# Two open heads' sums in the last periods, eight fill halves a period, a sixth early heads' step, half routing pieces, and two late weights in free buffers

## The chip, the cores and the metric

The kernel runs on one core of a Trainium2 chip. The metric is the device time of one execution in microseconds. TensorE is PE here, VectorE DVE, ScalarE ACT, GpSimd POOL; SP is the queue that issues the DMAs. PE reads its operands from SBUF and writes the eight PSUM banks, each of 128 x 512 float32: three score banks st0 to st2, four banks sm0 to sm3, and one bank dn.

## The reference

Input x has 2048 tokens of 512 features. Two branches are mixed by a gate per token:

```python
g = sigmoid((x * gate_w).sum(-1, keepdims=True))
qkv = (x @ wqkv).reshape(B, S, 3, 32, 16).transpose(2, 0, 3, 1, 4)     # 32 heads of 16
p = softmax(einsum("bhqd,bhkd->bhqk", q, k) * 16 ** -0.5)
a = merge(einsum("bhqk,bhkd->bhqd", p, v)) @ wo                         # attention
b = (sigmoid(x @ w_gate) * (x @ w_up)) @ w_down                         # GLU, 1792 hidden
out = g * a + (1 - g) * b
```

## The kernel before

Every matrix product is made of three matmuls on high and low parts of the operands (`terms`), which makes it exact enough in the fast number format. The instructions of PE, ACT, DVE and POOL run in the order in which the program writes them; SP's order is set by a scheduler.

The main loop (L891) has 256 periods, numbered k. In each, PE does eight score matmuls (`st_part`, L679, four "t0" for the period and four "t1" for the next), whose exponentials ACT takes (L681), eight matmuls for the row maxima of later scores (L292, "m0", "m1"), which DVE reduces (L294), twelve halves of a "fill" sum, and at the end the values (`values`, L831): probabilities times v, 16 records in the trace. The bank of the values is copied by ACT, in the last eleven periods by DVE (L838), and POOL adds the copy to a running sum (L848). A string of words, STEADY, gives the order in a period.

A fill sum (class `Sum`) is work that has nothing to do with the scores: the GLU's products, and towards the end the **early heads' steps**. A sum's operands have 128 rows, but each matmul of it takes only 64 of them, the lower or the upper half of PE's rows ("d0" and "d1"), so that it runs beside a score matmul, which uses the other half of the rows. [...]

From k = 245 on no row maxima are left, and the order is

```python
LAST = "t0 d1 t0 d1 t0 d1 turn t0 t1 t1 d0 t1 d0 t1 d0"
```

six halves a period. Scores and values take their banks from a ring of seven (`bank7`), the open fill sum is in dn, and DVE copies finished sums out (L469). There are EARLY = 5 steps of the last projection (attention output times wo) of which the first half of the heads, k-chunks 0 and 1 of 4, is summed in this way: ten sums of 12 halves, stored as `hp` (L515) and loaded back in the final stage.

Beside this, three more things hang in the main loop. The routing logits (`logits`, L818): 16 DVE instructions of 128 x 512, each multiplying 128 rows of x with the gate weights and summing, two in every six periods from k = 75 to 122; the rows of x are loaded by `logit_load` (L814). The denominators (L789 reciprocals on DVE), one in each period from k = 192 to 211. The first two chunks of the GLU's gate (`hidden_early`, L757), exponentials on ACT in k = 242 to 245.

The final stage (from L1011) is the GLU's down projection: 28 chunks of 24 matmuls (L1021) at about 0.227 us, four banks at a time (`bankt`, the first is dn), with eight heads' steps between them (`heads_out`): 4 k-chunks for steps that were not begun early, 2 for those that were. The values of k = 255 stand behind the first 12 down matmuls. The weights w_down are loaded late (`late_raw`), two row blocks at a time into a ring of two buffers, and split into high and low parts by ACT and POOL (L101, L104; `wd_h`, `wd_l`).

Of the kernel before, what the change touches and what calls it, by code (L numbers as in the profile page):

```python
# [12 lines left out]
F32 = mybir.dt.float32  # L13
# [25 lines left out]
FREE = NPER - LEAD // 2  # L39
EARLY = 5  # L40
WARM = 9
# [5 lines left out]
def gated_mix(ctx, tc, x, xT, wqk, wv, wo, w_gate, w_up, w_down, gate_w, out):  # L47
# [103 lines left out]
    class Sum:  # L151


        def __init__(self, o, ab):
            self.o, self.n, self.last, self.token = o, 0, None, None
            self.ops = list(terms(ab))
            self.left = [list(self.ops), list(self.ops)]
# [230 lines left out]
    def filling():  # L388
# [87 lines left out]
        def sums_of(kind, n, ws):  # L476
# [93 lines left out]
        for job, nxt in zip(jobs, jobs[1:]):  # L570
            kind, n = job
            coming = None
            for at, run in enumerate(sums_of(kind, n, ws)):
# [7 lines left out]
                if job == ("chain", pairs[-1]):  # L581
# [3 lines left out]
                    if at in (6, 7):  # L585
                        first_heads_split(at - 6)
                if kind == "heads" and at in (2, 4, 6):
                    if at == 2:
                        first_heads_load(4)
                    first_heads_split(at // 2 + 1)  # L590
# [126 lines left out]

    def late_raw(src, r):
        raw = keep.tile([P, 2, D], F32, name=f"late{r}", tag="ev", bufs=2)
        sp.dma_start(raw, src[r * P:(r + 2) * P, :].rearrange("(k p) d -> p k d", p=P))  # L720
        return raw

    def down_late(f, raw):
        if f < 6:
            th, tl, bufs = ("wh", "wl", 4) if f < 4 else ("sum", "part", 2)
            for a in range(2):
                if f + a == 5:
                    th = tl = "wr"
                h = keep.tile([P, D], F32R, name=f"wd{f + a}h", tag=th, bufs=bufs)
                l = keep.tile([P, D], F32R, name=f"wd{f + a}l", tag=tl, bufs=bufs)  # L730
                split(h, l, raw[:, a, :], act, pool)
                wd.append((h, l))
        else:
            fs = slice(f - 6, f - 4)
            split(wd_h[:, fs, :], wd_l[:, fs, :], raw, act, pool)
            wd.extend((wd_h[:, f - 6 + a, :], wd_l[:, f - 6 + a, :]) for a in range(2))
# [78 lines left out]

    def logits(t, a):
        xn = tok[t][:, a, :]
        dve.tensor_tensor_reduce(xn, xn, gwb, scale=1.0, scalar=0.0, op0=ALU.mult, op1=ALU.add,  # L818
                                 accum_out=logit[:, t + a:t + a + 1])

# [31 lines left out]
    def mx(b):  # L852
        for j in range(LEAD, NSTEP):
# [6 lines left out]
            denominators(1, 32, 64, 2)]  # L860
    run = next(fill)

    def dense(g):
        while run:
            run.half(g)
            yield

    spot = []

    def emit(order, **parts):  # L870

        for word in order.split():
            if word == "turn":
                if run:
                    turn(run)
# [8 lines left out]
    SUMS = 0  # L884
    LAST = "t0 d1 t0 d1 t0 d1 turn t0 t1 t1 d0 t1 d0 t1 d0"

# [4 lines left out]
    for k in range(NPER):  # L891
        n = 2 * k
        if n + LEAD == NSTEP:
            bank = bank7
            leave = dve.tensor_copy
        if 75 <= k < 123:
# [13 lines left out]
        if run and run.done():  # L910
            run = next(fill, None)
        elif run and run.n:
            turn(run)
        for half in list(mrow):
            later[:0] = put_max(half)
        work(2.6)
        later.extend(soon)
# [158 lines left out]
```

## Time and profile before

| | |
|---|---|
| median of 3 runs | 1687.64 us (1687.16 to 1688.01) |
| profiled execution | 1688.48 us |
| its span in the trace | 1686.7 us |
| TensorE clock granted | 0.999 |
| PE, DVE, ACT, POOL busy | 100%, 86%, 81%, 56% of the span |

The span runs from the first to the last recorded instruction; 1.78 us of the execution lie around it. Starts and durations in the rows of the trace are in us from the span's start. In a row such as `514.70 1.91 PE L831 MATMUL sm<-p,v ... x16`, the first number is the start, the second how long it (or the run of 16 alike) took, and `sm<-p,v` says that a bank of the sm kind is written from the tiles p and v.

### The profile page before, as it was taken

Reading aid. Unit: us, or ns where it says so; the run is one execution under the profiler, and the core shown is the slowest. Engines: PE = TensorE matmul, PEld = TensorE weight load, DVE = VectorE, ACT = ScalarE, POOL = GpSimd, SP = SyncE. Lnnn points to the kernel's source line nnn. Section 1 sums busy time; section 2 is a strip of 40 time slices with the busy share of each in tenths; the row PEclk is TensorE's granted clock in tenths of the full one; section 3 lists DMA queues with packets and bytes.
Section 4 is the critical chain, followed back from the end, with each engine's and each line's share of the span. In section 5 each row is a group of like instructions: output and inputs, shape, how many; then the busy total and the mean of one; then the engine's idle time right before and its main releaser. Section 6 shows DMA issues by size and latency. Waiting matters only on the chain.

```text
span 1686.7 us, 34636 instructions
## 1 busy us (share of the span) xinstructions
PE 1679.6 (100%) x12485; PEld 1027.2 (61%) x12485; DVE 1451.5 (86%) x2347; ACT 1362.6 (81%) x2657; POOL 938.9 (56%) x920
## 2 busy tenths in 40 slices
PE   9999999999999999999999999999999999999999
PEld 7755555555555555555555555555555555568887
DVE  7988888888889999999888888889998888787653
ACT  4188898988988898889898888989888988985331
POOL 1134476647666666566666766666666667543110
PEclk9999999999999999999999999999999999999999
DMA  7511457366565554555635353434343535368862
GB/s 237 148 46 59 127 175 210 133 164 208 145 197 133 166 156 151 163 162 182 165 102 146 102 145 107 137 104 132 104 129 113 133 110 171 109 208 285 290 200 70
DMA packets 143755, 254.19 MB, mean 151 GB/s; under 512 B 24224, under 2 KB 36512, under 8 KB 140704
## 3 DMA queue, kind: packets, MB, share of 16 engines
q1 hardware_dynamic: 135968, 237.30, 46.6%
q10 hardware_dynamic: 7616, 14.68, 2.8%
q8 instruction: 98, 1.61, 0.4%
q14 instruction: 73, 0.60, 0.1%
HBM read 149.42 MB, written 102.50 MB: 149 GB/s over the span
## 4 chain that ended last, share of the span: by engine, by line
PE 97%; DMA 1%; POOL 1%; issue 0%; ACT 0%; DVE 0%; SPq 0%; POOLq 0%; DVEq 0%
PE dn L162 30%; PE sm L831 27%; PE sm L292 13%; PE st L679 7%; PE sm L679 5%; PE sm L1021 4%; PE st L292 2%; PE st L162 2%; PE dn L1021 2%; PE st L1021 1%; PE st L643 1%; PE st L149 1%; PE sm L149 1%; DMA late<-in_w_down_dram 0%; PE st L831 0%
## 5 line engine op out<-in xcount | busy, mean ns | idle before, releaser
L294 DVE TENSOR_REDUCE stat<-sm 128x1 f32<-128x512 f32 x1313 | 848.6, 681 | 142.3 <-PE sm L679 127.9
L681 ACT ACTIVATE p<-st 128x512 f32<-128x512 f32 x1019 | 616.6, 650 | 1.1 <-PE st L679 0.6
L681 ACT ACTIVATE p<-sm 128x512 f32<-128x512 f32 x1027 | 609.6, 630 | 0.8 <-PE sm L679 0.5
L292 PE MATMUL sm<-ks,qs 48*128 48x512 f32 x1313 | 515.8, 435 | 0.1
L831 PE MATMUL sm<-p,v 128*17 128x512 f32 x4016 | 480.0, 595 | 0.0
L294 DVE TENSOR_REDUCE stat<-st 128x1 f32<-128x512 f32 x735 | 479.5, 680 | 0.1
L679 PE MATMUL sm<-qs,ks 64*128 64x512 f32 x1027 | 427.5, 419 | 0.0
L679 PE MATMUL st<-qs,ks 64*128 64x512 f32 x1019 | 425.8, 418 | 0.2 <-ACT p L681 0.2
L292 PEld LDWEIGHTS sm<-ks,qs 48*128 48x128 f32 x1313 | 234.0, 184 | 291.3 <-DVE stat L294 211.4
L848 POOL TENSOR_TENSOR sum<-sum,part 128x512 f32<-128x512 f32 x224 | 288.8, 1289 | 135.5 <-PE sm L679 121.1
L292 PE MATMUL st<-ks,qs 48*128 48x512 f32 x735 | 290.1, 395 | 0.0
L831 PEld LDWEIGHTS sm<-p,v 128*17 128x17 f32 x4016 | 93.2, 96 | 225.8 <-issue 155.4
L836 ACT ACTIVATE part<-sm 128x512 f32<-128x512 f32 x214 | 128.3, 599 | 126.2 <-issue 85.9
L542 POOL TENSOR_TENSOR chain<-chain,chain 128x512 f32<-128x512 f32 x96 | 124.1, 1293 | 156.2 <-PE sm L679 144.7
L679 PEld LDWEIGHTS st<-qs,ks 64*128 64x128 f32 x1019 | 187.5, 184 | 30.2 <-issue 3.4
L679 PEld LDWEIGHTS sm<-qs,ks 64*128 64x128 f32 x1027 | 189.4, 185 | 9.8 <-issue 5.1
L542 POOL TENSOR_TENSOR had<-chain,had 128x512 f32<-128x512 f32 x96 | 123.6, 1288 | 40.2 <-PE sm L679 17.2
L292 PEld LDWEIGHTS st<-ks,qs 48*128 48x128 f32 x735 | 137.2, 187 | 1.2 <-ACT v L662 0.3
L607 ACT ACTIVATE chain<-dn 128x512 f32<-128x512 f32 x128 | 88.2, 689 | 0.0
L542 POOL TENSOR_TENSOR side<-side,side 128x512 f32<-128x512 f32 x32 | 41.4, 1293 | 77.8 <-PE sm L679 69.7
L104 POOL TENSOR_TENSOR ol<-ot,oh 128x512 fp32r<-128x512 f32 (+1 forms) x8 | 14.7, 1843 | 103.7 <-ACT oh L101 103.7
L319 POOL CAST mhl<-mt 128x32 fp32r<-128x32 f32 x32 | 7.6, 237 | 103.9 <-DVE mt L300 103.9
(913 smaller groups left out, 3226.0 us busy)
## 6 DMA issues: line engine op xcount, KB each, us to landing
gul<-gu_d SPq DMA_DIRECT2D x56, 512.0 KB
had<-gu_d SPq DMA_DIRECT2D x84, 256.0 KB
gu_d<-had SPq DMA_DIRECT2D x84, 256.0 KB
gu_d<-side SPq DMA_DIRECT2D x56, 256.0 KB
pv_d<-sum SPq DMA_DIRECT2D x32, 256.0 KB
qs<-q_d SPq DMA_DIRECT2D x30, 256.0 KB
ks<-k_d SPq DMA_DIRECT2D x30, 256.0 KB
gu_d<-far SPq DMA_DIRECT2D x28, 256.0 KB
```

What stands on the lines that cost most here:

```text
L149: pe.matmul(o, a, b, start=(i == 0), stop=(i == len(ops) - 1))
L162: mm = pe.matmul(self.o, a[rows], b[rows], start=(self.n == 0), stop=(self.n == 2 * len(self.ops) - 1))
L292: pe.matmul(t, qs[r:r + KM, qt * P:(qt + 1) * P], ks[r:r + KM, g * 512:(g + 1) * 512], start=True, stop=True)
L294: dve.tensor_reduce(stat[half][:, b, qt % 8, g:g + 1], t, axis=AX.X, op=ALU.max)
L542: pool.tensor_tensor(to, u, w, ALU.add)
L607: leave = lambda e, o: act.activation(e, o, AF.Copy)
L679: pe.matmul(o, ks[r:r + KR, (kt + a) * P:(kt + a + 1) * P], qs[r:r + KR, q0:q0 + 512], start=True, stop=True)
L681: act.activation(pt[:, 2 * a + c, :], o, AF.Exp, scale=DH ** -0.5)
L831: pe.matmul(o[32 * c:32 * c + VW, :], v[:, 2 * k % 16 + a, h * VW:(h + 1) * VW], pts[c // 2][:, 2 * a + c % 2, :], start=(a == 0), stop=(a ...
L836: act.activation(e, o, AF.Copy)
L848: pool.tensor_tensor(s, s, e, ALU.add)
L1021: pe.matmul(down[t], a, b, start=(f == 0 and m == 0), stop=(f == NF - 2 and m == 5))
```

## The change

- EARLY goes from 5 to 6: two more fill sums, and 12 matmuls fewer in the final stage (792 instead of 804 there).
- In the last eleven periods two sums may be open, in the banks sm3 and dn in turn; the upper halves of a sum come first, and its lower halves only when all its upper ones are done, so a sum has one turn. LAST has eight halves a period. The ring of scores and values has six banks. What remains of the last sum after k = 255 is run alone.
- The routing logits are made in halves of 256 columns, one in each of four of six periods (r = 2 to 5 instead of whole ones in r = 3 and 4), and one DVE addition joins them later.
- The denominators run over k = 192 to 214 and skip k%8 = 4.
- The gate's exponentials run one period earlier, in k = 241 to 244.
- w_down's row blocks 6 to 9 get buffers of their own ("er"), and four late loads are out ahead instead of two.

The diff, cut to its core:

```diff
-EARLY = 5
+EARLY = 6
-    logit = keep.tile([P, NS], F32, name="logit")
+    logit = keep.tile([P, 2, NS], F32, name="logit")
...
                         run = Sum(bankd(), [((oh[:, k, cols], ol[:, k, cols]), ws[k]) for k in range(2)])
+                        run.end = lambda run=run, u=u, a=a: sp.dma_start(hp_d[2 * u + a], out_of(run, f"hp{u}_{a}"))
                         yield run
-                        sp.dma_start(hp_d[2 * u + a], out_of(run, f"hp{u}_{a}"))
...
-    bank7 = turns([seven[b] for b in (5, 1, 6, 2, 3, 4, 0)])
...
     def late_raw(src, r):
+        if src is w_down and r in (6, 8):
+            raw = [keep.tile([P, D], F32, name=f"late{r + a}", tag="er", bufs=6) for a in range(2)]
+            for a in range(2):
+                sp.dma_start(raw[a], src[(r + a) * P:(r + a + 1) * P, :])
+            return raw
...
-    def logits(t, a):
-        xn = tok[t][:, a, :]
-        dve.tensor_tensor_reduce(xn, xn, gwb, scale=1.0, scalar=0.0, op0=ALU.mult, op1=ALU.add,
-                                 accum_out=logit[:, t + a:t + a + 1])
+    def logits(t, a, i):
+        cols = slice(256 * i, 256 * i + 256)
+        xn = tok[t][:, a, cols]
+        dve.tensor_tensor_reduce(xn, xn, gwb[:, cols], scale=1.0, scalar=0.0, op0=ALU.mult, op1=ALU.add,
+                                 accum_out=logit[:, i, t + a:t + a + 1])
...
-    run = next(fill)
+    running = [next(fill)]
 
     def dense(g):
-        while run:
-            run.half(g)
+        while True:
+            if running and n + LEAD >= NSTEP and not running[-1].left[1] and len(running) < 2:
+                running.extend(filter(None, [next(fill, None)]))
+            for run in running:
+                if run.left[g] and (g == UP or n + LEAD < NSTEP or not run.left[UP]):
+                    run.half(g)
+                    if g == UP and not run.left[g] and n + LEAD >= NSTEP:
+                        turn(run)
+                    break
             yield
...
-    LAST = "t0 d1 t0 d1 t0 d1 turn t0 t1 t1 d0 t1 d0 t1 d0"
+    LAST = "t0 d1 t0 d1 t0 d1 t0 d1 turn t1 d0 t1 d0 t1 d0 t1 d0"
...
-            bank = bank7
+            bank = turns([seven[b] for b in (5, 1, 6, 2, 4, 0)])
+            bankd = turns([seven[3], dn])
             leave = dve.tensor_copy
...
-            if r in (3, 4):
-                logits(2 * t, r - 3)
+            if r >= 2:
+                logits(2 * t, *divmod(r - 2, 2))
...
+        if k == NPER - 1:
+            while running:
+                next(parts["d0"])
+                if running[0].done():
+                    close()
...
-        if NPER - 15 < k <= NPER - 11:
+        if NPER - 16 < k <= NPER - 12:
             for _ in range(2):
                 next(next(exps))
...
-        if 192 <= k < 212:
+        if 192 <= k < 215 and k % 8 != 4:
             next(dens[0], None)
...
-    loaded.extend(hidden_load(*chunks[m]) for m in range(2, 6))
-    act.activation(g1, logit, AF.Sigmoid)
+    loaded.extend(hidden_load(*chunks[m]) for m in range(2, 4))
+    raws.extend(late_raw(*late[m][:2]) for m in range(2, 4))
+    loaded.extend(hidden_load(*chunks[m]) for m in range(4, 6))
+    dve.tensor_tensor(g1, logit[:, 0], logit[:, 1], ALU.add)
+    act.activation(g1, g1, AF.Sigmoid)
...
-            if len(late) > 1:
-                raws.append(late_raw(*late[1][:2]))
+            if len(late) > 3:
+                raws.append(late_raw(*late[3][:2]))
```

PE in the last periods, before: from the first score of k = 254 to its values (the banks in turn are sm3, st0, sm0, st1, sm1, st2, sm2, sm3, and the values write st0).

```order
L679 MATMUL sm3_72<-qs1_102,ks1_103 128x512
L162 MATMUL dn_68<-wo1h_16884,xh_107 128x512 [waits Pool_sequencer_49]
L679 MATMUL st0_65<-qs1_102,ks1_103 128x512
L162 MATMUL dn_68<-wo1l_16885,xh_107 128x512
L679 MATMUL sm0_69<-qs1_102,ks1_103 128x512 [waits Activation_49]
L162 MATMUL dn_68<-wo1h_16884,xl_108 128x512
L679 MATMUL st1_66<-qs1_102,ks1_103 128x512 [waits Activation_49]
L679 MATMUL sm1_70<-qs1_102,ks1_103 128x512 [waits Activation_49]
L679 MATMUL st2_67<-qs1_102,ks1_103 128x512 [waits Activation_49]
```

The same stretch of the change, the first five scores of k = 254 with their fill halves; the values of k = 254 write sm0 there.

```order
L679 MATMUL sm2_71<-qs1_102,ks1_103 128x512
L162 MATMUL dn_68<-wo0h_16898,xh_107 128x512 [waits DVE_49]
L679 MATMUL st0_65<-qs1_102,ks1_103 128x512 [waits Activation_49]
L162 MATMUL dn_68<-wo0l_16899,xh_107 128x512
L679 MATMUL sm0_69<-qs1_102,ks1_103 128x512 [waits Activation_49]
L162 MATMUL dn_68<-wo0h_16898,xl_108 128x512
L679 MATMUL st1_66<-qs1_102,ks1_103 128x512 [waits Activation_49]
L162 MATMUL dn_68<-wo1h_16900,xh_107 128x512
L679 MATMUL sm1_70<-qs1_102,ks1_103 128x512 [waits Activation_49]
```

The bank of the values moved from that of the second score to that of the third, every score has a half beside it, and the wait for POOL (the turn), which stood before one or two halves of each period, stands once in each sum.

PE from the values of k = 254 to the first down matmul (L1021 before, L1053 after; in the L1021 rows xh and xl hold the first GLU chunk, in the L162 rows the attention output of the heads), before:

```order
L831 MATMUL st0_65<-p254_0_18111,v_99 17x512
L679 MATMUL sm0_69<-qs1_102,ks1_103 128x512
L679 MATMUL st1_66<-qs1_102,ks1_103 128x512
L679 MATMUL sm1_70<-qs1_102,ks1_103 128x512 [waits Activation_49]
L679 MATMUL st2_67<-qs1_102,ks1_103 128x512 [waits Activation_49]
L1021 MATMUL dn_68<-wd0h_17439,xh_107 128x512 [waits DVE_49]
```

And after:

```order
L679 MATMUL st2_67<-qs1_102,ks1_103 128x512 [waits Activation_49]
L679 MATMUL sm2_71<-qs1_102,ks1_103 128x512 [waits Activation_49]
L162 MATMUL dn_68<-wo0h_16898,xh_107 128x512 [waits Pool_sequencer_49]
L162 MATMUL dn_68<-wo0l_16899,xh_107 128x512
L162 MATMUL dn_68<-wo0h_16898,xl_108 128x512
L162 MATMUL dn_68<-wo1h_16900,xh_107 128x512
L162 MATMUL dn_68<-wo1l_16901,xh_107 128x512
L162 MATMUL dn_68<-wo1h_16900,xl_108 128x512
L1053 MATMUL dn_68<-wd0h_17455,xh_107 128x512 [waits DVE_49]
```

Six halves stand alone between the last score and the first down matmul, on the bank that the latter writes.

DVE at the same place, before (part is the copy of the values' bank, hp that of a heads' sum, gul, xh and xl the GLU's first chunk and its parts):

```order
L469 COPY hp4_1_18137<-dn_68 128x512 [waits DMAHW4_49,DMAHW1_49,PE_49]
L838 COPY part254_18148<-st0_65 128x512 [waits PE_49,Activation_49,Pool_49]
L774 TENSOR_TENSOR xl_108<-gul0_2_17384,xh_107 128x512 [waits DVE_49]
L772 CAST xh_107<-gul0_2_17384 128x512
L774 TENSOR_TENSOR xl_108<-gul0_2_17384,xh_107 128x512 [waits DVE_49]
L749 TENSOR_TENSOR gul0_4_18167<-gul0_4_18167 128x1024 [waits DMAHW4_49,Activation_49]
```

And after:

```order
L469 COPY hp5_0_18171<-sm3_72 128x512 [waits DMAHW3_49,PE_49]
L847 COPY part254_18182<-sm0_69 128x512 [waits PE_49,Activation_49,Pool_49]
L782 TENSOR_TENSOR xl_108<-gul0_2_17400,xh_107 128x512 [waits DVE_49]
L780 CAST xh_107<-gul0_2_17400 128x512
L782 TENSOR_TENSOR xl_108<-gul0_2_17400,xh_107 128x512 [waits DVE_49]
L469 COPY hp5_1_18210<-dn_68 128x512 [waits DMAHW6_49,PE_49]
```

The copy of the last heads' sum, which empties dn, stands behind the four instructions that follow the copy before it.

More of the change, by code (lines that the diff above doesn't have):

```diff
@@ L154, in __init__ @@
         def __init__(self, o, ab):
-            self.o, self.n, self.last, self.token = o, 0, None, None
+            self.o, self.n, self.last, self.token, self.end = o, 0, None, None, None
             self.ops = list(terms(ab))
@@ L586, in filling @@
                         first_heads_split(at - 6)
-                if kind == "heads" and at in (2, 4, 6):
-                    if at == 2:
-                        first_heads_load(4)
+                if kind == "heads" and at in (2, 4, 6, 8):
+                    if at < 6:
+                        first_heads_load(at // 2 + 3)
                     first_heads_split(at // 2 + 1)
@@ L734, in down_late @@
             fs = slice(f - 6, f - 4)
-            split(wd_h[:, fs, :], wd_l[:, fs, :], raw, act, pool)
+            if f < 10:
+                for a in range(2):
+                    split(wd_h[:, f - 6 + a, :], wd_l[:, f - 6 + a, :], raw[a], act, pool)
+            else:
+                split(wd_h[:, fs, :], wd_l[:, fs, :], raw, act, pool)
             wd.extend((wd_h[:, f - 6 + a, :], wd_l[:, f - 6 + a, :]) for a in range(2))
@@ L860, in gated_mix, with close @@
             denominators(1, 32, 64, 2)]
-    run = next(fill)
+    running = [next(fill)]
     def dense(g):
-        while run:
-            run.half(g)
+        while True:
[7 more added lines that the diff above has]
+                    break
             yield
+    def close():
+        run = running.pop(0)
+        if run.end:
+            run.end()
     spot = []
@@ L873, in emit @@
             if word == "turn":
-                if run:
-                    turn(run)
+                if running and n + LEAD < NSTEP:
+                    turn(running[0])
                 work(2.0)
@@ L909, in gated_mix @@
         emit(STEADY if k < FREE else LAST, **parts)
[L910 to L913, printed above, removed]
+        if running and running[0].done():
+            close()
+            if n + LEAD < NSTEP:
+                running.extend(filter(None, [next(fill, None)]))
+        elif running and n + LEAD < NSTEP:
+            turn(running[0])
         for half in list(mrow):
@@ L916, in gated_mix @@
         work(2.6)
+        if k == NPER - 1:
+            while running:
+                next(parts["d0"])
+                if running[0].done():
+                    close()
         later.extend(soon)
```

## Prediction

> **What bounds the kernel now.** I read the page first: the engines' shares and the chain that ended last.
>
> ```profile
> PE 1679.6 (100%) x12485; PEld 1027.2 (61%) x12485; DVE 1451.5 (86%) x2347; ACT 1362.6 (81%) x2657; POOL 938.9 (56%) x920
> PE 97%; DMA 1%; POOL 1%; issue 0%; ACT 0%; DVE 0%; SPq 0%; POOLq 0%; DVEq 0%
> ```
>
> PE is the bound nearly everywhere, so a gain can come from three things only: fewer matmuls, or places where another engine holds PE back, or an interval between periods that another engine sets. The timeline of PE, read at the values' matmuls (16 records a period), shows such intervals.
>
> ```profile
> 514.70 1.91 PE L831 MATMUL sm<-p,v 128*17 128x512 f32 x16
> 520.28 1.91 PE L831 MATMUL sm<-p,v 128*17 128x512 f32 x16
> 526.25 1.05 PE L831 MATMUL sm<-p,v 128*17 128x512 f32 x8
> ...
> 694.30 1.91 PE L831 MATMUL sm<-p,v 128*17 128x512 f32 x16
> ...
> 700.16 1.91 PE L831 MATMUL sm<-p,v 128*17 128x512 f32 x16
> ```
>
> An ordinary period takes 520.28 - 514.70 = 5.58 us; the one with a routing piece takes 5.97, so 0.39 is lost. Of the 16 intervals with a piece, four are longer than 5.58 in this way, by 0.28 to 0.39, and the last of them is 700.16 - 694.30 = 5.86: 1.29 us together.
>
> **Routing pieces.** The timelines of DVE and POOL at two pieces, and at a place where a half will stand:
>
> ```profile
> 521.87 1.25 DVE L818 CUSTOM_DVE_ANT_0 xn<-xn,gwb 128x512 f32<-128x512 f32 x1
> ...
> 523.06 0.68 DVE L294 TENSOR_REDUCE stat<-sm 128x1 f32<-128x512 f32 x1
> ...
> 527.85 0.67 DVE L818 CUSTOM_DVE_ANT_0 xn<-xn,gwb 128x512 f32<-128x512 f32 x1
> ...
> 528.62 0.69 DVE L294 TENSOR_REDUCE stat<-sm 128x1 f32<-128x512 f32 x1
> ...
> 534.20 0.69 DVE L294 TENSOR_REDUCE stat<-sm 128x1 f32<-128x512 f32 x1 [0.71 <-PE sm L292]
> ```
>
> ```profile
> 521.85 0.72 POOL L448 TENSOR_TENSOR side_8r<-side_8r 128x256 f32<-128x256 f32 x1
> ...
> 527.87 1.26 POOL L448 TENSOR_TENSOR side_1r<-side_1r,side_8r 128x256 f32<-128x256 f32 x1
> ...
> 533.41 1.29 POOL L136 TENSOR_TENSOR sq<-sq 128x512 fp32r<-128x512 f32 x1
> ...
> 751.98 1.29 POOL L136 TENSOR_TENSOR sq<-sq 128x512 fp32r<-128x512 f32 x1
> ```
>
> Eight reduces fill 523.06 to 527.85, 0.60 each, so a period of 5.58 leaves DVE 0.78. The piece at 527.85 holds it 0.77 (to 528.62): free. The piece at 521.87 holds it 1.19, and 1.19 - 0.78 = 0.41 is the 0.39 lost. In the first, POOL began 0.02 earlier; in the second DVE was first, and POOL's operation, 0.72 elsewhere, took 1.26. [...]
>
> What a half costs no row shows. Bounds: 0, and the full 0.77. The nearest row is the piece at 527.85, 0.67 of work and 0.10 up to the next reduce (0.77 - 0.67): half the columns would hold DVE 0.10 + 0.33 = 0.43, well inside the 0.78. The present losses go: **-1.3**. But halves stand in four of six periods, also where DVE had been free (the 0.71 idle before 534.20), and there POOL starts its 1.29 at 533.41, while DVE comes free at 534.20 - 0.71 = 533.49. A half that loses that draw ends near 533.41 + 1.29 + 0.40 = 535.1, 0.9 after the next reduce should have begun. Going through POOL's operations at the places of all 32 halves, six stand in one already begun (the first at 533.41, the last at 751.98), with 0.64 to 1.28 left (0.2 to 0.8 lost each, 2.6 in all), and four more tie. Since a shift of 0.1 decides most, I take half of the six: **+1.3**, with 0 to 5.9 (2.6 + 4 x 0.82) as ends. The rows of x are also needed one period earlier. Only the second load is near its use:
>
> ```profile
> 545.59 0.38 SPq L814 DMA_DIRECT2D xn<-in_x_dram x1
> 548.57 1.91 PE L831 MATMUL sm<-p,v 128*17 128x512 f32 x16
> 1510.44 7.89 DMA late<-in_w_down_dram
> ```
>
> Issued at 545.59, used at 548.57 + 1.6 = 550.2: 4.6 us for 512 KB, where another load of 512 KB took 7.89 in the chain. Late by 0 to 3.3; I take 1.5, of which DVE's 0.3 left over hides some: **+1.2**. Pieces together: +1.2 (-1.3 to +7).
>
> **Denominators.** The slots of k%8 = 4 lie behind the transposes:
>
> ```profile
> 1230.43 1.91 PE L831 MATMUL sm<-p,v 128*17 128x512 f32 x16
> ...
> 1236.48 1.91 PE L831 MATMUL sm<-p,v 128*17 128x512 f32 x16
> ```
>
> ```profile
> 1232.70 0.55 DVE L789 RECIPROCAL den<-den 32x64 f32<-32x64 f32 x1
> ```
>
> That period took 6.05, 0.47 over; the other such one lost 0.13. Both are skipped, and the reciprocals land in periods that have 0.78 free: **-0.6** (0 to -0.6).
>
> **The last eleven periods.** PE's and ACT's timelines and the chain:
>
> ```profile
> 1470.13 2.00 PE L831 MATMUL st<-p,v 128*17 128x512 f32 x16
> ...
> 1472.40 0.39 PE L679 MATMUL st<-qs,ks 64*128 64x512 f32 x1
> ...
> 1474.05 0.62 PE L831 MATMUL st<-p,v 128*17 128x512 f32 x4
> ```
>
> ```profile
> 1473.15 0.83 ACT L681 ACTIVATE p<-st 128x512 f32<-128x512 f32 x1
> ```
>
> ```profile
> 1460.45 0.79 ACT L757 ACTIVATE gul<-gul 128x256 f32<-128x256 f32 x2
> ```
>
> The values of 1474.05 write the bank of the second score after the values before (1472.40) and start 0.07 after its exponential ends (1473.98). 1474.05 - 1470.13 = 3.92, which is eight exponentials at 0.49, and ACT runs without a gap there, so ACT sets the pace. With six banks in the ring the values take the bank of the third score. The loop then is: values 1.84 to 1.93, 0.60 until the first score is written, two exponentials at 0.48, 0.61 for the third, 0.07: 4.08 to 4.17. That is 0.2 more than 3.92, ten times: +2.0 to +2.5. Against it, the two pieces at 1460.45 (0.79) leave for a period that PE bounds and where ACT has room: up to -0.5. The two more fill halves run beside scores on the other half of the rows, as the six do: 0. Sum **+1.9** (-0.5 to +2.6).
>
> **Drain.** The timelines of PE, DVE and POOL where the GLU's down projection begins:
>
> ```profile
> 1493.70 1.95 PE L831 MATMUL st<-p,v 128*17 128x512 f32 x16
> ...
> 1496.71 0.50 PE L1021 MATMUL dn<-wd0h,xh 128*128 128x512 f32 x1
> ```
>
> ```profile
> 1496.40 0.68 DVE L774 TENSOR_TENSOR xl<-gul,xh 128x512 fp32r<-128x512 f32 x1
> 1497.00 1.53 DVE L772 CAST xh<-gul 128x512 fp32r<-128x512 f32 x1
> 1498.57 0.69 DVE L774 TENSOR_TENSOR xl<-gul,xh 128x512 fp32r<-128x512 f32 x1
> ```
>
> ```profile
> 1496.64 1.61 POOL L848 TENSOR_TENSOR sum<-sum,part 128x512 f32<-128x512 f32 x1 [2.25 <-PE sm L679]
> ```
>
> Before, the first down matmul follows the values of k=254 by 1496.71 - 1493.70 = 3.01. After, six halves of the last heads' sum come first, alone (6 x 0.23 = 1.4), and the first down matmul writes dn only when DVE has copied that sum out. The copy stands behind the three DVE rows above, which end 5.5 after the values (1498.57 + 0.6 - 1493.70); with 0.69 for it and 0.1 to PE, 6.25. Queued behind that wait on PE are all down matmuls and the values of k=255; on SP the sum's store, which waits for the same copy, stands ahead of four loads of late weights, which still go out near 1500 and so ahead of 1510.44. So **+3.2**; if the cast is not held up, it ends 1.1 earlier, and the sum's own end (4.5) plus copy decides: +2.4; if the copy meets another hold, +3.7. [...]
>
> **Final stage.** PE, the chain, and the window of 20 us (columns: busy time of PE, weight loads, DVE, ACT and POOL, PE's clock, DMA's share and GB/s):
>
> ```profile
> 1515.24 0.39 PE L1021 MATMUL dn<-wd_h,hl 128*128 128x512 f32 x1
> 1515.74 0.50 PE L1021 MATMUL dn<-wd_l,hl 128*128 128x512 f32 x1
> ...
> 1521.09 0.39 PE L1021 MATMUL dn<-wd_h,hl 128*128 128x512 f32 x1
> 1521.94 0.50 PE L1021 MATMUL dn<-wd_l,hl 128*128 128x512 f32 x1 [0.46 <-POOL wd_l L104]
> 1522.27 0.63 PE L1021 MATMUL dn<-wd_h,hl 128*128 128x512 f32 x2
> ```
>
> ```profile
> 1536.98 2.72 PE sm L1021 x12
> ```
>
> ```profile
> 1500.00:1520.00 20.00, 19.89 (x96) 15.14 (x89) 16.67 (x11) 11.67 (x15) 12.41 (x7) 1.00 1.00 335
> ```
>
> The sixth heads step needs 12 matmuls fewer here, and twelve take 2.72: **-2.7**. PE waits for the split of a late weight before 1515.74 and 1521.94: (0.50 + 0.85 - 2 x 0.23) and 0.1 after each, 1.1. Those weights now load ahead, into free buffers, and PE comes 3 us later: **-1.1** (0 to -1.1). The sixth step's load and split fall in steady periods where POOL is 56% busy: 0, or at most the 1.29 of one split that delays a routing piece, which the pieces' range holds. The gate's exponentials of one period earlier need loads that are issued in time for that: 0.
>
> **Sum:** +1.2 - 0.6 + 1.9 + 3.2 - 2.7 - 1.1 = +1.9 on the profiled execution's 1688.48, which is 1690.4. That execution lay 0.84 above the median of the three runs, 1687.64; against the median, 1689.5. A measurement of this kernel can tell about 0.2%, 3.4 us.
>
> **Rivals.** [...] The mechanism is the one of 521.87, in its place; the price is 2.6 + 1.3 (part of the ties) + 1.5 in place of the 1.3 + 1.2 above, +3 more: 1692.5. From six lost draws with a tie or two, and the load 1.5 late, the time is past 1691. For it: at all six POOL is ahead; against: at five of them by 0.1 or less, and only four of the 16 pieces before lost anything. 0.20. (2) Slower, and the change does not do what it says: from 1500 to 1520 the DMA engines are busy all the time (share 1.00), and two more sums to store and load back (4 x 256 KB at 335 GB/s, 3.1 us) push the other loads back, so that the down projection waits for them as long as the 12 matmuls took: +1.9 + 2.7 = +4.6, 1692.2. For it: the full share; against: all its waits on loads sum to 1.1 now. 0.10. (3) Faster: the values' bank is not what they wait for, so the last periods cost -0.5, no half loses a draw (-1.3), and dn comes free at +2.4: -0.5 - 1.3 - 0.6 + 2.4 - 2.7 - 1.1 = -3.8, so 1683.8. For it: every one of these is a bound that some row allows; against: it needs all three. 0.13. (4) The forecast, 1689.5, within 1687 to 1691: 0.57.
>
> So faster by over 0.2% (below 1684.3) has 0.13, within 0.57, slower (above 1691.0) 0.30. The range 1684.5 to 1693.0 leaves out part of (3) and the far end of (1).
>
> **What would show it.** In the changed profile: intervals between values in k 75 to 125 mostly 5.58, a few 5.8 to 6.4, with a POOL operation on two inputs beside each; DVE waiting for the x rows once near 550; no 6.05 near 1236; intervals near 4.1 in the last ten periods, each ended by the third score's exponential; PE idle for about 1.7 us before the first down matmul, released by DVE's copy of a heads sum; no wait on wd_l. I am wrong if the last intervals stay at 3.9, if dn comes free with the sixth half, or if the halves cost PE nothing.

## The result, and the profile after

| | before | changed |
|---|---|---|
| median of 6 runs | 1687.94 us (1687.16 to 1689.3) | 1695.8 us (1694.62 to 1697.62) |
| profiled execution | 1688.48 us | 1695.12 us |
| its span | 1686.7 us | 1693.3 us |

The changed kernel takes 1.0047 times as long, with an interval of 1.0036 to 1.0057: slower by 7.9 us, and above the top of the stated range, 1693.0. The spans differ by 6.6. The page of the changed kernel shows a first sign: in the chain that ended last, DVE now has a share of 3%, where it had none.

```profile
PE 1683.0 (99%) x12497; PEld 1028.0 (61%) x12497; DVE 1466.5 (87%) x2384; ACT 1364.5 (81%) x2659; POOL 944.6 (56%) x925
PE 96%; DVE 3%; DMA 1%; issue 0%; POOL 0%; DVEq 0%; SPq 0%; POOLq 0%
```

The starts of the values cut both traces at the same points of the program, so that their differences add up. Times are us between the values of the two k:

| stretch | before | changed | difference | forecast |
|---|---|---|---|---|
| start to k = 75 | 509.12 | 508.50 | -0.62 | 0 |
| 75 to 125 (routing pieces) | 280.42 | 286.97 | +6.55 | +1.2 |
| 125 to 190 | 362.63 | 362.66 | +0.03 | 0 |
| 190 to 220 (denominators) | 168.02 | 167.36 | -0.66 | -0.6 |
| 220 to 243 | 128.34 | 128.31 | -0.03 | 0 |
| 243 to 254 (last periods) | 45.17 | 46.38 | +1.21 | +1.9 |
| 254 to 255 (drain) | 5.96 | 10.53 | +4.57 | +3.2 |
| 255 to the end | 187.04 | 182.6 | -4.4 | -3.8 |

The change touches nothing in the first row; it is how far two executions differ there. The routing pieces and the drain carry the loss. The timelines of PE (the values, and the matmul after its longest wait), DVE, POOL and SP at the second load of x, k = 83:

```profile
548.07 1.91 PE L840 MATMUL sm<-p,v 128*17 128x512 f32 x16
...
551.18 0.39 PE L162 MATMUL dn<-xl,side(0, 1)h 64*128 64x512 f32 x1
553.08 0.49 PE L292 MATMUL sm<-ks,qs 48*128 48x512 f32 x1 [1.52 <-DVE stat L294]
...
556.96 1.91 PE L840 MATMUL sm<-p,v 128*17 128x512 f32 x16
```

```profile
551.44 0.98 DVE L827 CUSTOM_DVE_ANT_0 xn<-xn,gwb 128x256 f32<-128x256 f32 x1 [1.70 <-POOL sq L139]
552.35 0.08 DVE L827 DVE_READ_ACCUMULATOR2_ANT logit<- 128x1 f32 x1
552.35 0.68 DVE L294 TENSOR_REDUCE stat<-sm 128x1 f32<-128x512 f32 x1
```

```profile
550.86 1.28 POOL L136 TENSOR_TENSOR sq<-sq 128x512 fp32r<-128x512 f32 x1
```

```profile
545.16 0.43 SPq L822 DMA_DIRECT2D xn<-in_x_dram  x1
```

The interval is 556.96 - 548.07 = 8.89, 3.31 over 5.58. DVE waited 1.70 before the half at 551.44. The row names POOL's cast, but that had ended at 550.77; the packets of the load issued at 545.16 end at 551.32 in the trace, 0.12 before the half starts. (In the trace before, the same load, issued at 545.59, ended at 552.00, where nobody waited for it yet.) POOL was by then at work on its operation of 550.86, which ends at 552.14, and the half took 0.98, where the one at k = 84, with no POOL operation beside it, took 0.42; the next reduce starts at 552.35. The reduces behind it came late, and PE had nothing to do from 551.4 to 553.1. That wait is not all. Windows of 1 us (columns as in the prediction's window: five engines' busy time, PE's clock, DMA's share, GB/s) show what PE did after it:

```profile
552.00:553.00 1.00, 0.00 (x0) 0.00 (x0) 1.00 (x4) 0.16 (x1) 0.14 (x1) 1.00 0.56 170
...
554.00:555.00 1.00, 1.00 (x7) 1.00 (x7) 1.00 (x3) 0.96 (x2) 1.00 (x1) 0.50 0.61 137
555.00:556.00 1.00, 1.00 (x8) 1.00 (x7) 1.00 (x2) 0.80 (x3) 0.07 (x1) 0.50 1.09 297
```

PE's clock, 1.00 while it waited, was 0.50 from 553.60 to 557.01, and the matmuls into dn followed each other at 0.43 (554.11, 554.54, 554.97) where it had been 0.23 before the wait (550.49, 550.72, 550.95). The same happened in the drain:

```profile
1500.18 1.91 PE L840 MATMUL sm<-p,v 128*17 128x512 f32 x16
...
1504.20 0.39 PE L162 MATMUL dn<-wo1h,xl 64*128 64x512 f32 x1
1506.36 0.79 PE L1053 MATMUL dn<-wd0h,xh 128*128 128x512 f32 x1 [1.77 <-DVE hp L469]
1506.95 0.63 PE L1053 MATMUL dn<-wd0l,xh 128*128 128x512 f32 x1
1507.38 0.63 PE L1053 MATMUL dn<-wd0h,xl 128*128 128x512 f32 x1
...
1510.71 1.91 PE L840 MATMUL st<-p,v 128*17 128x512 f32 x16
```

```profile
1505.00:1506.00 1.00, 0.00 (x0) 0.00 (x0) 0.99 (x2) 0.98 (x1) 0.00 (x0) 0.96 1.00 256
1506.00:1507.00 1.00, 0.64 (x2) 0.55 (x3) 0.39 (x2) 0.58 (x2) 0.00 (x0) 0.50 1.00 361
1507.00:1508.00 1.00, 1.00 (x4) 0.81 (x3) 0.38 (x1) 1.00 (x2) 0.00 (x0) 0.50 1.05 408
```

DVE and POOL ahead of it:

```profile
1503.46 1.51 DVE L780 CAST xh<-gul 128x512 fp32r<-128x512 f32 x1
1505.01 0.69 DVE L782 TENSOR_TENSOR xl<-gul,xh 128x512 fp32r<-128x512 f32 x1
1505.62 0.68 DVE L469 COPY hp<-dn 128x512 f32<-128x512 f32 x1
```

```profile
1503.09 1.60 POOL L857 TENSOR_TENSOR sum<-sum,part 128x512 f32<-128x512 f32 x1 [2.46 <-PE st L679]
```

The cast, which takes 0.41 at 1501.10, takes 1.51 beside POOL's add, and DVE's copy out of dn ends at 1506.30, 0.06 before PE goes on. The first down matmul follows the values by 1506.36 - 1500.18 = 6.18, where the prediction had 6.25. The 12 down matmuls, from there to 1510.71, take 4.35 instead of 2.95 (1496.71 to 1499.66): 1.40 more, for the half clock.

Elsewhere between k = 75 and 125 the long intervals stand at r = 2: k = 77 (6.03), 89 (6.27), 95 (6.25), 107 (6.21), 113 (6.25), 119 (6.19), and 116 (6.08, r = 5). At k = 77 the half is late for another reason: it stands behind two small DVE operations of the row maxima (L298, L300) and starts 2.48 after the values instead of 1.59. At the others POOL is at work when DVE comes to the half, having started 0.02 to 0.17 ahead, and the half takes 1.38 to 1.55. This is the one of k = 89, by the timelines of PE, DVE and POOL:

```profile
584.92 1.91 PE L840 MATMUL sm<-p,v 128*17 128x512 f32 x16
...
591.19 1.05 PE L840 MATMUL sm<-p,v 128*17 128x512 f32 x8
```

```profile
586.52 1.55 DVE L827 CUSTOM_DVE_ANT_0 xn<-xn,gwb 128x256 f32<-128x256 f32 x1
```

```profile
586.50 1.29 POOL L136 TENSOR_TENSOR sq<-sq 128x512 fp32r<-128x512 f32 x1
```

POOL starts 0.02 ahead, and the half, 0.42 elsewhere, takes 1.55. In the last periods the intervals are 4.06:

```profile
1487.99 1.91 PE L840 MATMUL st<-p,v 128*17 128x512 f32 x16
...
1492.06 1.03 PE L840 MATMUL sm<-p,v 128*17 128x512 f32 x5
```

### The profile page after: what moved, and what is told of

It is laid out like the page before. It is cut to its first block, busy times and chain, and to the rows that moved or that the text cites. A ratio compares the mean times of both kernels' runs of the same rounds, so it can differ in the third digit from the quotient of the medians.

```text
span 1693.3 us, 34710 instructions
## 1 busy us (share of the span) xinstructions
PE 1683.0 (99%) x12497; PEld 1028.0 (61%) x12497; DVE 1466.5 (87%) x2384; ACT 1364.5 (81%) x2659; POOL 944.6 (56%) x925
## 4 chain that ended last, share of the span: by engine, by line
PE 96%; DVE 3%; DMA 1%; issue 0%; POOL 0%; DVEq 0%; SPq 0%; POOLq 0%
PE dn L162 29%; PE sm L840 26%; PE sm L292 12%; PE st L679 7%; PE sm L1053 5%; PE sm L679 5%; DVE stat L294 2%; PE dn L1053 2%; PE st L292 2%; PE st L162 2%; PE st L1053 2%; PE st L643 1%; PE st L149 1%; PE st L840 1%; PE sm L149 1%; DVE xn L827 1%
## 5 line engine op out<-in xcount | busy, mean ns | idle before, releaser
L681 ACT ACTIVATE p<-sm 128x512 f32<-128x512 f32 x1022 | 602.5, 621 | 5.1 <-PE sm L679 4.9
```

The source lines that it names most:

```text
L681: act.activation(pt[:, 2 * a + c, :], o, AF.Exp, scale=DH ** -0.5)
```

## The experiments

**The theory** after these readings: (a) the second load of x is late, and PE's wait for it costs twice, once as a wait and once as half clock; (b) the halves at r = 2 stand where POOL's operation delays DVE's (1.55 instead of 0.42 at k = 89); (c) in the drain PE waits for dn and then again runs at half clock; (d) the six banks give 4.06. No run shows what DVE and POOL share at (b); where an expectation says "the port", it is a name for these delays. In each expectation, theory A is what follows from these points and B its rival. The runs were made in three groups, each on one chip, and ratios are to the kernel before in the same group: 1687.63 us for e1_load_early, e2_keep_busy, e3_shift and e4_free_bank; 1688.47 for e1b_second_load, e7_one_input, e8_shift_free and e5_early5; 1687.96 for the last four.

**e1_load_early**

```diff
-            if r == 1:
+            if r == 0:
                 logit_load(2 * t)
```

> The changed kernel, with the rows of x for the routing pieces asked for one period earlier (r = 0 instead of r = 1). In the changed kernel the interval to the values of k = 83 was 8.89 us, 3.31 over 5.58. Theory A: DVE's piece waits 1.7 us there for the second load, the reduces behind it hold PE for 1.5 us, and PE then runs for about 3 us at half clock; with the load there in time the interval falls to 5.6 (the piece is free) or 6.2 (it loses the draw for the port as at k = 89), so the time falls by 2.7 to 3.3, to about 1692.8. Rival B: the interval is long because the load's own traffic or POOL's operation beside it holds DVE; then an earlier load moves the loss to another period and the time stays within 1 us of 1695.8.

Measured: 1696.43 us, ratio 1.0052 (1.0039 to 1.0064), the interval at k = 83 again 8.88. This did not test the theory: SP's timeline shows that the load did not go out earlier. It stood behind the same other transfer and left at the same place of the period.

```profile
545.39 0.38 SPq L806 DMA_DIRECT2D sq<-s_d  x1
546.27 0.38 SPq L822 DMA_DIRECT2D xn<-in_x_dram  x1
```

What follows is that a request placed earlier in the program is not a load placed earlier on SP's queue. Since the kernel behaves as the changed one does, its 1696.43 serves as a repeat of it in this group.

**e2_keep_busy**

```diff
+            if (n, t) == (0, 0):
+                for _ in range(8):
+                    pe.matmul(maxb[3], ops[0][0], ops[0][1], start=True, stop=True)
             for m, (a, b) in enumerate(ops):
```

> The changed kernel with eight matmuls more: before the first down matmul PE writes eight products of operands that it has already (128 rows, 512 columns, 0.227 us each, 1.8 us in all) into the bank sm3, which nobody reads; the result is unchanged. In the changed kernel PE stands idle there for 1.8 us, and the next seven matmuls follow each other at 0.43 us instead of 0.227 with a granted clock of 0.50. Theory A: the idle time itself lowers the clock; with PE kept busy the clock stays at 1.00, the wait ends when it did, the 12 down matmuls take 2.8 to 3.0 instead of 4.35, and the time falls by about 1.4, to 1694.4. Rival B: the slow matmuls come from the DMA traffic beside them (share 1.00 in that window); then they stay slow and the time stays, or rises by what the added matmuls overlap, 0 to 0.3.

Measured: 1693.53 us, 1.0035 (1.0023 to 1.0048), 2.9 less than the repeat, with eight matmuls more. PE's timeline and a window:

```profile
1505.93 2.11 PE L1054 MATMUL sm<-wd0h,xh 128*128 128x512 f32 x8
1507.88 0.40 PE L1056 MATMUL dn<-wd0h,xh 128*128 128x512 f32 x1
1508.11 0.40 PE L1056 MATMUL dn<-wd0l,xh 128*128 128x512 f32 x1
```

```profile
1508.00:1509.00 1.00, 1.00 (x6) 0.82 (x5) 0.00 (x0) 1.00 (x3) 0.00 (x0) 1.00 1.06 410
```

The wait for dn is still there (6.30 after the values), but the clock stays at 1.00 with DMA as busy as before (share 1.06, 410 GB/s), and the 12 down matmuls take 2.83 (1507.88 to 1510.71). The drain's interval is 9.13 instead of 10.53, 1.4 less as expected. So traffic of this size did not lower the clock here (the changed kernel has 0.50 at a share of 1.05 and 408 GB/s); what differs ahead of it is that PE had work while it waited. The rest of the 2.9 is within the spread of these five runs (1690.33 to 1695.53).

**e3_shift**

```diff
-            if r >= 2:
-                logits(2 * t, *divmod(r - 2, 2))
+        if 78 <= k < 126:
+            t, r = divmod(k - 78, 6)
+            if r < 4:
+                logits(2 * t, *divmod(r, 2))
```

> The changed kernel with the routing halves one period later (r = 3, 4, 5 and the next r = 0 instead of r = 2 to 5). All the long intervals of the changed kernel but one stand at r = 2 (k = 77, 83, 89, 95, 101, 107, 113, 119), together 7.2 us over 5.58. Theory A: there POOL's operation on the sq tile (1.29 us, two inputs) starts when the half should, and the second load of x is late; elsewhere the halves are nearly free. Then the time falls by 6 to 7.2, to about 1689.0. Rival B: a half costs PE wherever it stands, since the doubled number of pieces meets POOL as often at other places; then the losses move to r = 0 and the time falls by the late load's 3.3 at most, to 1692.5.

Measured: 1689.02 us, 1.0009 (1.0000 to 1.0018), 7.4 under the repeat: theory A. From k = 75 to 125 it takes 279.83 (changed 286.97, before 280.42). Of the long intervals 116 (5.99) and 78 (5.73) are left; the halves at r = 0 cost nothing in their own periods. In this execution the drain took 9.13 without anything done for it: PE's wait for dn was the same 1.76, but the clock stayed up. So the half clock after a wait of this length came in two executions (1.77, changed; 1.76, e1_load_early) and not in this one (1.76).

**e4_free_bank**

```diff
-    bankt = turns([dn, maxb[1], banks[2], maxb[2], maxb[3]])
+    bankt = turns([maxb[3], maxb[1], banks[2], maxb[2], dn])
```

> The changed kernel with the down projection beginning in bank sm3, which is free by then, and dn last in its ring of five. Theory A: from the values of k = 254 to those of 255 the changed kernel takes 10.53 us where the kernel before takes 5.96; of these 4.57, 1.4 are the six halves alone, 1.8 the wait for DVE's copy out of dn, and 1.4 the half clock after it. With a free bank the wait and the clock go: 7.3 to 7.5 us, and the time falls by 3.2, to 1692.6. Rival B: behind the wait for dn stands another that ends at nearly the same time, DVE's xl of the same chunk (it ended at 1505.7, 0.6 before the copy); then only 0.6 of the wait goes, PE still stands idle for over 1 us, and the time falls by 0.6 to 1.

Measured: 1693.07 us, 1.0027 (1.0017 to 1.0037), 3.4 under the repeat: theory A. PE, from the values of k = 254:

```profile
1498.95 1.91 PE L840 MATMUL sm<-p,v 128*17 128x512 f32 x16
...
1502.98 0.39 PE L162 MATMUL dn<-wo1h,xl 64*128 64x512 f32 x1
1503.30 0.50 PE L1053 MATMUL sm<-wd0h,xh 128*128 128x512 f32 x1
...
1506.24 0.63 PE L840 MATMUL st<-p,v 128*17 128x512 f32 x4
```

The down projection begins 0.32 after the last half, and the drain takes 7.29. What is left over 5.96 is the six halves alone, 1.3. This execution is the fastest of its eight; the clock held at k = 83 too.

**e1b_second_load**

```diff
-            if r >= 2:
+            if t != 1 and r >= 2:
                 logits(2 * t, *divmod(r - 2, 2))
+        if 84 <= k < 88:
+            logits(2, *divmod(k - 84, 2))
```

> The changed kernel with the four halves of the second load of x (k = 83 to 86) one period later (k = 84 to 87), all others where they were. The run before this one asked for the load a period earlier, and it went out at the same place all the same, so this moves the use instead. Theory A: the interval of 8.89 at k = 83 is the wait for this load (the piece started when the load had landed, 1.7 us late) and the clock after it; with the use one period later it falls to 5.6, and so the time by 2 (in executions where the clock had held) to 3.3, to 1692.5 to 1693.8. Rival B: the slot of r = 2 there is long by POOL's operation on sq like those of k = 89 and 95; then 0.7 of it goes.

Measured: 1692.47 us, 1.0020 (1.0011 to 1.0029), with 5.58 at k = 83:

```profile
549.07 1.91 PE L840 MATMUL sm<-p,v 128*17 128x512 f32 x16
554.65 1.91 PE L840 MATMUL sm<-p,v 128*17 128x512 f32 x16
```

From 75 to 125 it takes 283.77, 3.2 less than the changed kernel. Theory A: the interval of k = 83 is the late load.

**e7_one_input** (each half sums its columns of x without the gate weights, so the gate comes from other numbers)

```diff
-        dve.tensor_tensor_reduce(xn, xn, gwb[:, cols], scale=1.0, scalar=0.0, op0=ALU.mult, op1=ALU.add,
-                                 accum_out=logit[:, i, t + a:t + a + 1])
+        dve.tensor_reduce(logit[:, i, t + a:t + a + 1], xn, axis=AX.X, op=ALU.add)
```

> The changed kernel with the halves left in their places, but each only sums its 256 columns of x (a reduce with one SBUF input) without the product with the gate weights, so that the gate is computed from other numbers. Theory A: a DVE operation with two SBUF inputs has to wait for POOL's, one with a single input has not; then the intervals of r = 2 at k = 77, 89, 95, 107, 113, 119 and of 116 fall from 6.0 to 6.3 to 5.6, together 4.2 us less, and k = 83 keeps its late load (2 to 3.3 over): about 1691.6. Rival B: DVE has too little time in these periods for any half, whatever its inputs; the intervals stay, and the time is within 1 us of 1695.8.

Measured: 1690.28 us, 1.0010 (1.0001 to 1.0018). DVE and POOL at k = 89:

```profile
585.00 0.41 DVE L827 TENSOR_REDUCE logit<-xn 128x1 f32<-128x256 f32 x1
```

```profile
584.97 1.29 POOL L136 TENSOR_TENSOR sq<-sq 128x512 fp32r<-128x512 f32 x1
```

POOL is ahead by 0.03, much as in the changed kernel, yet the half takes 0.41, and the interval is 5.58. All seven long intervals are at 5.65 or less; only k = 83, the late load, stays long (7.02, in an execution whose clock held there). Theory A, in that DVE does not lack the time: the product with two SBUF inputs took 1.55 beside POOL's operation, and this sum of one input takes 0.41. The run changed the operation together with its inputs, and one input alone is no safeguard: the cast of the drain has one and took 1.51 instead of 0.41 beside POOL's add. So which of the two decides is not shown.

**e8_shift_free** (the edits of e3_shift and e4_free_bank together)

> The changed kernel with the halves at r = 3, 4, 5 and the next 0 and with the down projection beginning in the free bank sm3. Theory A: the two savings add: 1689.0 with the shift alone, less the 1.8 of the wait for dn, and less the half clock in those executions that had it: 1686.5 to 1687.2, at or a little below the kernel before. Rival B: the loads of the final stage set its end, and what is saved before it is lost there to waits for loads: within 0.5 of 1689.0.

Measured: 1686.56 us, 0.9989 (0.9980 to 0.9997): the savings add, and this is faster than the kernel before, by 1.9 us in the same group. The list of PE's waits for other engines has no entry after the first microseconds.

**e5_early5** (with the edit of e3_shift, and without the sixth step's load and split)

```diff
-EARLY = 6
+EARLY = 5
...
```

> The changed kernel with five early heads' steps as before (ten sums) and with the halves at r = 3, 4, 5 and 0, the rest as in the change. With eight halves a period the ten sums end before the last period, so nothing is left to run alone and dn is free. Theory A: the sixth step as built costs more than it brings: from the values of k = 254 to those of 255 it takes 9.13 instead of 5.96 without the clock, 3.2, for 12 matmuls of 2.7 in the final stage; so this is 0.5 faster than the 1689.0 of the shift alone, and less spread. Rival B: the final stage waits for its loads as soon as PE comes to it earlier, as it did before the change (1.1 us of waits for the late weights), so this is 0.5 to 1 slower, about 1689.8.

Measured: 1688.46 us, 0.9998 (0.9989 to 1.0007), beside 1.0009 of e3_shift in another group. By these ratios it is the faster of the two by 1.9; by the two profiled executions, whose clock held, it is the slower by 0.2. The drain falls from 9.13 to 5.91, but the final stage grows from 182.6 to 186.2, more than the 2.7 of theory A. No wait for a late weight, as B had it, stands in the trace. So the size that A gave, 0.5, is not shown. Beside e8_shift_free in the same group it is 1.9 slower: the sixth step is worth its place once the drain is free of the wait.

**e6_before_halves** (the kernel before with only the halves of the change)

> The kernel before with one part of the change alone: the routing halves at r = 2 to 5. Theory A: this part makes the change slow by itself; against the kernel before, the second load of x costs 2 to 3.3 and the halves beside POOL 4.6 more, less the 1.3 that the whole pieces lost: +5.3 to +6.6, 1693.0 to 1694.2 where the kernel before has 1687.6. Rival B: the halves are only slow together with the other parts, for example because the earlier steps' loads shift POOL's operations; then this is near the kernel before, within 2.

Measured: 1694.18 us, 1.0036 (1.0023 to 1.0050): theory A. k = 83 takes 9.50 here, and the same intervals are long at r = 2. One part alone carries 6.2 of the 7.9.

**e9_before_six**

```diff
-    bank7 = turns([seven[b] for b in (5, 1, 6, 2, 3, 4, 0)])
+    bank7 = turns([seven[b] for b in (5, 1, 6, 2, 4, 0)])
```

> The kernel before with a ring of six banks instead of seven for scores and values in the last periods (bank sm3 unused), all else as it was. Theory A: the values then take the bank of the third score, the loop through its exponential sets the period, and the last ten intervals go from about 3.93 to 4.06, as in the change: 1 to 1.5 slower, about 1688.8. Rival B: what made 4.06 in the change is the two halves more in each period; then the intervals stay near 3.93 here and the time at 1687.6.

Measured: 1689.49 us, 1.0008 (0.9999 to 1.0017), 1.5 slower.

```profile
1470.46 1.91 PE L831 MATMUL sm<-p,v 128*17 128x512 f32 x16
...
1474.52 1.91 PE L831 MATMUL st<-p,v 128*17 128x512 f32 x16
```

The intervals are 4.06 with six halves a period as with eight, and the stretch from 243 to 254 takes 46.75 instead of 45.17: +1.6. Theory A: the ring's size sets them.

**e10_without_last** (the kernel before with halves at r = 3, 4, 5, 0, the denominators and the late weights of the change)

> The kernel before with the parts of the change that do not touch the last periods: halves at r = 3, 4, 5 and the next 0, denominators that skip k%8 = 4, and the late weights in free buffers with four loads ahead; five early steps, seven banks and six halves a period as before. Theory A: each gives what the change's trace showed or should have given: 1.3 less 0.5 for the halves, 0.6, and 1.1 for the waits on late weights, so about 1685.3, faster than all kernels so far. Rival B: without a later start of the down projection the final stage waits for its loads again, and the 1.1 is not gained: about 1686.4, like the change with shift and free bank.

Measured: 1687.43 us, 0.9996 (0.9987 to 1.0004): not told apart from the kernel before, and neither expectation is met. In its profiled execution, the fastest of its 11, no wait for late weights is left (nor is there one in e6_before_halves and e9_before_six, which have the loads of the kernel before), and the denominators' two long intervals are gone. But from 125 to 190 it takes 363.38 where the kernel before takes 362.63: as in all kernels with the halves at r = 0, intervals of 5.7 to 5.8 stand at k = 148, 158, 177, 187 and 216, which lie behind the pieces. In e3_shift the operations of DVE and POOL start at the same distance from the values, within 0.03, in k = 158, 187 and 216 as in the changed kernel, so it is not these two that hold PE there; where these intervals come from is open. Of theory A's terms they take back the halves' gain, and the 1.1 was not there to be had (see the final stage below).

**e11_exps_too** (e10_without_last with the gate's exponentials in k = 241 to 244)

> The kernel of the run before this one with the gate's exponentials one period earlier too (k = 241 to 244). Theory A: the interval of 4.33 at k = 246, which held two of them, falls to 3.93, and the ones at k = 241 are hidden behind PE: 0.4 less, about 1684.9. Rival B: ACT had been the bound in k = 245 and 246 only by a backlog that another period takes over, or DVE's work behind the exponentials comes to lie beside something else: no difference.

Measured: 1686.74 us, 0.9992 (0.9983 to 1.0000), 0.7 under e10_without_last. The stretch from 243 to 254 falls from 45.22 to 44.61: theory A in the difference, with 3.83 at k = 246 instead of 4.33; its 1684.9 stood on the 1685.3 that e10_without_last missed.

## Why the prediction was wrong, point by point

- **Routing pieces, +1.2, measured +6.55: the step that failed.** Both causes were the ones given, halves beside POOL's operation (1.55 instead of 0.42 at k = 89) and the late load, and 6.55 lies within the range given for this term (-1.3 to +7); what failed is the price chosen in it, half of the six places lost and no tie. Of the six places where POOL had begun before, two were lost (k = 116 and 119, 1.1); but all four ties were (k = 89, 95, 107, 113, 0.63 to 0.69 each, 2.7), and two places that were not on my list (k = 77 and 101, 0.6), where the half stands behind the small operations of the row maxima and not behind POOL. At r = 2 POOL starts a few hundredths before the half in one group of six periods after another, so the ties were not independent draws. That order stood in the trace before: at these four places POOL's operation starts 1.57 to 1.58 after the values (583.92 after 582.35 at k = 89), and a piece of DVE 1.59 (521.87 after 520.28). At the first of the six, k = 80, POOL stood at 1.59 as well (I took DVE as free at 533.49, by the end in its row, where 533.41 is the start that a piece would have had), and in the changed kernel it began 0.24 after the half. The intervals of k = 75 to 125 other than 83 lost 4.6; a half alone costs 0.42, as estimated, and is free where POOL is idle (5.57 and 5.58 at k = 84 and 96 of the changed kernel).
- **The second load, +1.2 in that sum.** It was late by 1.8 (half at 551.44, slot at 549.66), close to the 1.5 that I took, and it cost 3.31. What was missing is PE's half clock after its wait; without it, in e4_free_bank, the interval is 7.21, 1.63 over.
- **Drain, +3.2, measured +4.57.** The wait was right to 0.07 (6.18 against 6.25, on DVE's copy, behind the cast, which took 1.51 beside POOL's add and 0.41 without: 1.10 apart, the 1.1 of the forecast's lower case). The half clock after it, 1.40, was not in the sum: neither here nor at the second load does the prediction give a wait of PE anything but its length, and it gives no reason for that.
- **Last periods, +1.9, measured +1.21.** The mechanism holds (e9_before_six): the bank of the third score. The interval is 4.06 where the loop gave 4.08 to 4.17, so the ring costs 1.6 (e9_before_six) and not 2.0 to 2.5; the exponentials give back the 0.4 to 0.5 (e11_exps_too gained 0.6 in the trace).
- **Denominators, -0.6, measured -0.66.** Right.
- **Final stage, -2.7 - 1.1, measured -4.4.** The 12 matmuls are gone, and no wait for a late weight is left. But the 1.1 was an accident of the one profiled execution of before: in e6_before_halves and e9_before_six, whose final stage is the same, it takes 186.0 and 186.1 instead of 187.04, with no such wait. With the late weights of the change and five early steps it takes 185.6, 185.8 and 186.2 (e10_without_last, e11_exps_too, e5_early5), so the late weights bring 0.5 at most. From there to the 182.6 of the change the sixth step brings 3.0 to 3.6, more than its 12 matmuls at 2.7; where the rest comes from is open. The profiled execution of before lay 0.5 above its median of six and that of the change 0.7 below, so the medians differ by 7.9 and the spans by 6.6.
- **The rivals.** The time is beyond the first rival, 1692.5, whose causes it has: that price holds the six lost places, part of the ties and the late load, and no clock. Rival (2), that loads eat the gain of the final stage, was wrong (the stage gained 4.4), and so was (3).

In sum: +4.6 for the halves, most of it lost draws, and +3.3 for the late load, less 1.4 that the whole pieces had lost, make 6.55 where I had 1.2; 1.4 of clock in the drain; 0.7 less in the last periods.

## What to carry to other kernels

Operations of two engines that meet at a fixed point of a period are not drawn by lot: here POOL, ahead by 0.02 to 0.07 us, was ahead at all four ties, so such ties are to be counted as lost, or the operation is moved by a period, as in e3_shift. A wait of PE is priced with the clock that may follow it: here 1.68 us behind the wait of 1.52 at k = 83 (8.89 against 7.21 in e4_free_bank) and 1.40 behind that of 1.77 in the drain. If the wait can't go, work that nobody needs can be cheaper than idleness (e2_keep_busy: the drain 9.13 instead of 10.53). And a stall seen in one profiled execution, above its median, is not yet a gain to be had.

## What the runs showed of the hardware

In the changed kernel's trace the low records of the granted clock start at points of a grid: 0.50 from 553.60 to 557.01 and from 1505.92 to 1509.33, 3.413 us each, and again from 1693.65, behind the last matmul. The starts are 952.32 and 187.73 apart, 279 and 55 times 3.4133. In e1_load_early the starts are 555.06 and 1507.38, again 952.32 apart. Counted from the start of the span, the grid lies differently in each execution (553.60, 555.06 and, in e2_keep_busy, 555.67 leave 0.64, 2.10 and 2.71 over a multiple of 3.4133), so the same wait is split differently by it. Idle time of PE inside one stretch of the grid (counted from 0.23 after the start of the last matmul; the ends in the rows, which are modelled, give 0.16 less where the wait begins inside the stretch), and what followed: 1.68, 1.95, 2.08 and 2.30 at k = 83 (changed, e1_load_early, e2_keep_busy, e6_before_halves) and 1.50, 1.62, 1.71 and 1.93 in the drain (changed, e1b_second_load, e1_load_early, e7_one_input), half clock in the next stretch; 1.25 and 1.40 at k = 83 (e7_one_input, e4_free_bank) and 1.31 in the drain (e3_shift), full clock. At these two places 1.50 of 3.41 and more was followed by half clock, 1.40 and less was not. It is not one number of idle time everywhere: at the end of e4_free_bank, behind matmuls on all 128 rows, 1.92 were idle (1685.03 to 1686.95), more than in three of the four drains just named, and the clock stayed at 1.00 in the stretch that followed. At k = 83 and in the drains matmuls on 48 or 64 rows stand ahead of the wait; whether that makes the difference no run tests.

In e2_keep_busy the place of the drain's wait, 1505.85 to 1507.88, lies whole in one stretch (1504.58 to 1507.99, counted on from its low clock at 555.67), so it was the eight matmuls and not the grid's place that kept the clock up there. In e3_shift the wait crosses a border of the grid, at 1499.57.

The grid may be part of the spread of the changed kernel's runs (1694.62 to 1697.62, with two such waits); the kernel before, without them, also spreads over 2.1 us (1687.16 to 1689.3), so the runs do not show how much of it.
